# Linear attention and a cosine-gated feed-forward: Strassen's method in six token blocks instead of five, kv of two batches written by VectorE

## The chip, the cores and the metric

One NeuronCore of a Trainium2 chip. The metric is the device time of one launch in microseconds (us); the kernel before takes 818.85 us, the median of three runs (818.57 to 818.89).

## The reference

```python
def attention(q, k, v):                      # (8, 8, 576, 64): batch, head, row, d
    q_s = exp(q - max(q, -1));  q_s /= sum(q_s, -1) + 1e-9
    k_s = exp(k - max(k, 2));   k_s /= sum(k_s, 2) + 1e-9
    kv = einsum('bhsd,bhse->bhde', k_s, v)
    return einsum('bhsd,bhde->bhse', q_s, kv)

x = attention(q, k, v).transpose(0, 2, 1, 3).reshape(4608, 512)
h = x @ w_in                                 # 512 x 2048
return (h * cos(h)) @ w_out                  # 2048 x 512
```

All tensors are fp32.

## The kernel before, in words

**Tiling.** The 4608 token rows are cut into nine blocks of 512: block b = 0 to 7 holds the first 512 rows of batch b, block 8 the 64 rows left of each batch, which pass through the scratch tensor x_left. The 2048 hidden columns are 16 chunks f of 128. A block and a chunk make a unit u, 144 in all. Blocks 0 and 1 are done in turns of eight chunks (units 0 to 31); from block 2 on, u = 16 b + f.

**A unit.** fp32 operands are split into a high and a low part (type fp32r), so a product is three matmuls. A standard unit's h is 12 matmuls of 128 x 512 on TensorE (PE, L1215). Then come: ScalarE (ACT) `turns` L1221, VectorE (DVE) `rest` L1225, ACT cosine L1231, DVE `gate` L1237, ACT `hi` L1248, DVE `lo` L1254. Two units later 12 matmuls of 128 x 512 with w_out add into four PSUM banks (acc, L1458; L1451 for the first six units). w_in lies in SBUF as 16 tiles w_i (or w_io), high and low.

**Strassen.** In blocks from SB = 4 on, two units (u, u + 1) make a pair, and `products()` (from L1285) forms both h from seven products in Winograd's form, each of six matmuls of 128 x 256 (L1330). Products 0 and 1 go into the bank pb ("T1" and "B11"). ACT copies pb into the two halves of h (`seed`, L1349) and to SBUF (`p5_out`, L1353), and DVE adds p5 twice (`add_12` L1356, `add_22` L1359) between products: add_12 reads what product "T2" has finished and must read it before "T3" adds to the same half; add_22 stands between "T3" and "T4". `x_parts()` (from L919) makes the sums of x that the products need: minus L944, high and low parts L931 to L962. In a standard block x's low part is L1080.

**Sums of w_in.** `combine(a)` (from L1379) makes the sums of chunks 2a and 2a + 1: DVE L1397 to L1412, split by ACT L1416 and DVE L1420, and stores them with copies of the plain quarters in a DRAM tensor `combined` (L1389, L1391, L1424). The eight combines are listed from unit 32 on, one per four units. Each Strassen block loads 28 pieces of 512 KB back (L1298), two products per piece, into a ring of eight w_i tiles that are free by then.

**Attention.** For a batch b and a pair of heads p: k's softmax (L690 to L718), kv on PE (L767, 20 matmuls for one p), the reciprocal of its sums on DVE (L784, L787), then the 128 x 128 tile of two kv blocks. In batches 0 and 1, POOL zeroes the tile (L799) and ACT writes two 64 x 64 blocks (L804); in later batches DVE writes kvt in one instruction with a mask (`kv_norm`, L791), and ACT and DVE split it. x is PE L1044 with ACT L1058 and L1078 behind it.

**Order.** Every step goes into a plan, and the list ORDER (L59 on) is the order of all steps, written as numbers. Each engine and the DMA queue on SyncE (SP) works its own instructions in that order, and waits in it where data or a tile isn't ready. The h ring has two banks, the intermediate ring r2 three tiles.

Of the kernel before, what the change touches and what calls it, by code (L numbers as in the profile page):

```python
# [49 lines left out]
    SB=4,  # L50
# [9 lines left out]
0 1 2 3 12 4 31 7 28 13 14 20 21 80 8 9 81 74 82 15 16 83 75 24 25 34 76 84 35 85 10 11 142 77 36 78 26 27 37 44 79 45  # L60
5 6 38 92 46 86 47 29 30 94 42 52 39 48 22 23 143 40 87 49 160 161 105 54 88 41 55 50 144 311 312 313 93 43 64 56 89
106 57 95 96 97 17 18 19 156 51 98 32 33 90 100 65 53 58 101 99 66 179 180 107 59 91 67 108 330 331 102 72 162 319 109
117 157 317 318 320 112 60 321 119 68 322 110 118 163 61 323 130 145 69 328 62 314 315 316 111 324 70 63 146 113 203
204 71 120 325 334 158 121 147 73 164 326 181 159 332 122 165 114 125 123 355 356 357 131 333 126 338 182 132 347 339
358 359 124 133 327 127 166 340 148 183 341 134 149 137 167 342 335 140 141 135 184 138 336 337 343 185 150 139 136
205 349 350 186 151 344 360 168 223 224 206 243 244 361 329 173 174 152 345 207 362 153 351 208 187 366 353 369 370
363 154 367 368 169 155 209 364 192 225 352 196 197 346 354 365 193 103 104 348 287 288 194 226 210 263 264 377 170
175 216 217 211 227 188 256 257 379 228 171 189 378 229 172 190 380 230 176 381 191 231 382 177 245 383 212 198 213
302 303 246 178 195 115 116 371 384 199 236 237 202 214 789 790 247 265 385 248 266 513 514 200 218 579 580 201 249
128 129 388 267 222 389 783 784 785 372 219 232 215 278 279 220 250 552 553 373 221 390 391 268 238 251 233 392 374  # L70
269 394 270 242 395 375 234 376 289 258 393 290 235 252 291 398 239 253 271 400 292 254 240 259 241 399 280 255 401
# [12 lines left out]
853 636 681 652 667 682 1151 1152 1153 637 683 653 704 705 656 550 551 854 684 668 820 805 685 669 806 654 670 655 671
709 710 807 843 866 867 674 821 822 686 687 693 1466 1467 823 688 689 824 920 724 921 694 672 695 673 696 922 690 844
692 725 923 691 697 845 855 702 701 726 700 711 735 706 712 713 727 707 708 728 846 856 736 868 857 698 703 719 720
847 869 699 743 714 715 737 729 848 738 739 879 880 731 744 730 732 858 859 751 894 895 721 924 716 1160 717 718 745
881 882 733 1161 746 734 1162 752 747 1163 742 925 1164 753 1154 1155 1156 754 740 926 759 741 860 928 929 870 861 755
927 871 872 873 767 875 874 760 883 748 1165 896 897 750 876 1173 761 942 943 749 762 722 723 1174 768 758 884 930 931
769 756 885 825 763 886 757 764 887 1175 770 775 898 888 889 899 771 890 765 900 766 776 1180 1167 932 777 1176 933  # L90
778 1177 826 936 937 779 1157 901 1170 772 774 903 773 934 935 904 891 782 780 781 947 948 1171 1172 902 941 905 1168
1169 938 906 1178 939 1158 1159 1166 909 944 1181 1182 1179 945 946 962 910 911 1000 912 1001 940 913 963 952 953 1183
964 892 893 1002 965 949 914 1003 950 951 1004 973 1052 1053 915 1197 1208 954 1198 1199 966 957 958 969 974 1200 1201
981 967 975 1005 976 955 956 977 862 863 1184 989 968 982 959 983 960 961 1185 1211 1212 970 990 971 1006 991 984 972
1007 1186 980 1202 1010 1011 978 992 1012 985 877 878 1203 1014 1015 1019 986 979 993 987 1204 1013 1027 1020 1016
1017 1021 1187 1209 1210 1205 988 1028 1008 1009 1206 1188 1207 1022 1189 1054 1018 1219 1220 994 1055 1023 918 919
995 1234 1235 1056 1035 1024 1190 1057 1221 1222 1058 1059 1029 1060 1030 1061 1026 1512 1036 1031 1064 1065 1191 1025
1037 1513 1514 1043 1213 1038 1412 1413 1214 1034 1039 1044 1066 1032 1068 1069 1067 1045 1521 1073 1070 1071 1215
1223 1033 1104 1105 1216 1042 1236 1237 1046 1217 1040 1108 1074 1047 1041 1081 1048 1218 1062 1063 1075 1049 1264
1265 1072 1109 1082 1076 1110 998 999 1224 1111 1083 1249 1250 1112 1084 1080 1113 1192 1077 1114 1225 1115 1238 1118  # L100
1119 1089 1193 1194 1085 1251 1252 1086 1120 1226 1195 1227 1090 1097 1078 1091 907 908 1239 1079 1122 1123 1121 1240
1088 1124 1125 1098 1253 1092 1093 1116 1117 1196 1099 1127 1087 1094 1290 1291 1095 1096 1128 1522 1228 1100 1230
1231 1292 1126 1523 1101 1524 1129 1229 1130 1293 1294 1135 1131 1295 1132 1296 1133 1297 1241 1136 1242 1102 1143
1243 1103 1245 1244 1254 1137 1302 1246 1255 1134 1138 1518 1144 1515 1516 1517 1266 1267 1300 1301 1519 1520 1268
1525 1528 1298 1299 1534 1541 1139 1256 1145 1288 1289 1140 1257 1142 1535 1269 1304 1305 1141 1303 1146 1258 1306
1307 1147 1260 1536 1150 1259 1537 1148 1270 1286 1287 1538 1149 1531 1529 1530 1526 1271 1309 1542 1543 1273 1261
1362 1310 1315 1274 1272 1308 1275 1311 1276 1312 1363 1279 1313 1314 1539 1532 1533 1527 1540 1324 1280 1281 1364
1544 1282 1318 1283 1325 1319 1320 1284 1326 1232 1233 1365 1335 1327 1558 1569 1316 1317 1366 1285 1559 1560 1328
1561 1562 1343 1336 1329 1337 1572 1573 1367 1338 1330 1339 1331 1545 1332 1546 1333 1547 1344 1351 1321 1368 1322
1323 1369 1570 1571 1345 1563 1346 1334 1277 1278 1352 1342 1372 1373 1340 1353 1347 1354 1564 1374 1381 1341 1355  # L110
1375 1565 1574 1378 1379 1350 1348 1382 1349 1376 1377 1575 1414 1415 1389 1383 1247 1248 1416 1384 996 997 1566 1356
1370 1371 1380 1417 1390 1567 1385 1358 1359 1391 1576 1357 1106 1107 1397 1418 1656 1657 1419 1420 1548 1568 1392
1388 1549 1580 1581 1421 1393 1422 1577 1398 1658 1659 1386 1405 1578 1387 1582 1583 1423 1399 1396 1400 1406 1401
1394 1426 1427 1407 1550 1395 1408 1551 1424 1425 1435 1552 1579 1553 1618 1619 1409 1584 1404 1595 1596 1436 1554
1428 1402 1429 1585 1977 1437 1432 1433 1443 1438 1586 1597 1598 1403 1439 1555 1556 1451 1444 1470 1410 1978 1979
1471 1472 1473 1430 1431 1434 1474 1445 1411 1707 1708 1446 1475 1633 1634 1452 1447 1476 1453 1587 1440 1589 1477
1454 1459 1599 1480 1481 1482 1455 1600 1441 1662 1663 1986 1442 1460 1980 1981 1982 1987 1988 1483 1989 1601 1486
1487 1990 1450 1448 1620 1621 1449 1461 1557 1462 1991 1489 1456 1484 1485 1588 1463 1590 1457 1478 1479 1999 1602
1490 1604 1593 1458 1594 2000 1603 2001 1605 1491 1608 1622 1492 1497 1493 1635 1636 1623 1609 1464 1624 1610 1505
# [1592 lines left out]
```

## Time and profile before

| | |
|---|---|
| median of three runs | 818.85 us |
| profiled execution | 817.74 us |
| its span, first to last instruction | 816.0 us |
| PE busy | 794.2 us, 97% |
| DVE busy | 636.6 us, 78% |
| ACT busy | 536.1 us, 66% |
| POOL busy | 43.3 us, 5% |
| granted clock of PE | 1.000 of 2.4 GHz |

The profiled execution is one run of its own: 1.7 us of it lie outside the span, and it is 1.1 us shorter than the median of the other three. A table of windows gives each engine's busy time in a stretch; the ends used below are starts of blocks, as the trace has them (block 2 from 219.20, block 3 from 308.30, block 4 from 394.20, block 5 from 471.60 to 558.90 us). The waits view lists, for one engine, what ended its idle time. The chain is followed back from the last instruction.

### The profile page before, as it was taken

What the parts mean: (1) busy time and instruction counts of PE and PEld (TensorE: products, weight loads), DVE (VectorE), ACT (ScalarE), POOL (GpSimd) and SP (SyncE); (2) the same over time, 40 slices, a digit from 0 to 9 for tenths busy, and PEclk for the clock granted to TensorE, in tenths of its full rate; (3) what the DMA queues carried; (4) which work ended last, traced back from release to release, by engine and by line L of the source; (5) the groups of instructions that cost most, each with busy time, mean ns of one, the idle gap of its engine ahead of it and who ended that gap; (6) DMA issues with size and microseconds to landing.
All of it is one profiled execution on the core that took longest, in us unless ns stands there. A gap on an engine that the chain in (4) does not pass through costs nothing.

```text
span 816.0 us, 14069 instructions
## 1 busy us (share of the span) xinstructions
PE 794.2 (97%) x5028; PEld 706.4 (87%) x5028; DVE 636.6 (78%) x1108; ACT 536.1 (66%) x986; POOL 43.3 (5%) x161
## 2 busy tenths in 40 slices
PE   3899999999999999999999999999999999999997
PEld 2666888888888888888899999999999999999996
DVE  8999998888689886998787978687787646744444
ACT  5999998854656456756776767566666556645441
POOL 1300100000100020002000010002000000000000
PEclk9999999999999999999999999999999999999999
DMA  7893645535457544676889987998859665547721
GB/s 232 232 335 127 179 170 181 139 102 156 131 154 220 163 126 134 212 206 183 261 257 223 295 236 235 261 284 275 259 166 249 233 239 202 184 177 259 245 65 52
DMA packets 200070, 164.00 MB, mean 201 GB/s; under 512 B 110912, under 2 KB 172864, under 8 KB 200000
## 3 DMA queue, kind: packets, MB, share of 16 engines
q1 hardware_dynamic: 199680, 162.57, 66.0%
q8 instruction: 40, 0.66, 0.3%
q10 hardware_dynamic: 320, 0.52, 0.2%
q14 instruction: 30, 0.25, 0.1%
HBM read 128.71 MB, written 34.34 MB: 200 GB/s over the span
## 4 chain that ended last, share of the span: by engine, by line
PE 91%; DVE 3%; DMA 2%; SPq 1%; issue 1%; ACT 1%; POOL 0%; ACTq 0%; DVEq 0%; POOLq 0%
PE acc L1458 43%; PE h L1215 19%; PE h L1330 16%; PE pb L1330 6%; PE acc L1451 3%; PE x_False L1044 3%; PE kv L767 2%; DMA k<-in_k_dram 1%; DMA w_i<-combined 1%; POOL m L705 0%; DMA qload<-in_q_dram 0%; SPq L1093 0%; SPq L605 0%; SPq L624 0%; PE qt L995 0%
## 5 line engine op out<-in xcount | busy, mean ns | idle before, releaser
L1221 ACT ACTIVATE kt<-h 128x512 int32<-128x512 f32 x144 | 85.5, 596 | 119.4 <-PE h L1330 84.4
L1458 PE MATMUL acc<-w_o,ghi 128*128 128x512 f32 x504 | 150.1, 380 | 0.0
L1225 DVE SCALAR_TENSOR_TENSOR kt<-kt,h 128x512 f32<-128x512 int32 x144 | 97.9, 683 | 43.6 <-ACT kt L1221 43.1
L1215 PE MATMUL h<-x,w_i 128*128 128x512 f32 x528 | 121.7, 382 | 0.2 <-ACT x L1078 0.2
L1231 ACT ACTIVATE kt<-kt 128x512 f32<-128x512 f32 x144 | 90.0, 630 | 37.5 <-DVE kt L1225 36.8
L1215 PEld LDWEIGHTS h<-x,w_i 128*128 128x128 f32 x528 | 99.1, 189 | 15.4 <-ACT x L1078 0.6
L1237 DVE TENSOR_TENSOR kt<-kt,h 128x512 f32<-128x512 f32 x138 | 93.4, 684 | 23.5 <-ACT kt L1231 21.6
L1458 PEld LDWEIGHTS acc<-w_o,ghi 128*128 128x128 f32 x504 | 91.8, 190 | 11.0
L1458 PE MATMUL acc<-w_o,glo 128*128 128x512 f32 x252 | 95.5, 379 | 0.0
L1458 PE MATMUL acc<-w_o,w_io 128*128 128x512 f32 x360 | 91.4, 379 | 0.0
L1458 PE MATMUL acc<-w_io,ghi 128*128 128x512 f32 x280 | 83.4, 380 | 0.0
L1254 DVE TENSOR_TENSOR glo<-kt,ghi 128x512 fp32r<-128x512 f32 x98 | 67.3, 690 | 10.9 <-ACT ghi L1248 10.7
L1248 ACT CAST ghi<-kt 128x512 fp32r<-128x512 f32 x98 | 60.1, 617 | 21.5 <-PE acc L1458 10.7
L1458 PEld LDWEIGHTS acc<-w_o,w_io 128*128 128x128 f32 x360 | 64.3, 190 | 6.9
L1330 PE MATMUL h<-x,w_i 128*128 128x256 f32 x410 | 61.4, 275 | 0.8 <-DVE h L1356 0.5
L1330 PEld LDWEIGHTS h<-x,w_i 128*128 128x128 f32 x410 | 56.2, 191 | 3.2 <-DVE h L1356 0.7
L1330 PE MATMUL h<-w_i,w_i 128*128 128x256 f32 x358 | 57.2, 276 | 0.4 <-ACT h L1349 0.4
L1458 PEld LDWEIGHTS acc<-w_io,ghi 128*128 128x128 f32 x280 | 50.6, 190 | 5.8
L1215 PE MATMUL h<-x,w_io 128*128 128x512 f32 x240 | 55.0, 379 | 0.0
L1458 PEld LDWEIGHTS acc<-w_o,glo 128*128 128x128 f32 x252 | 47.6, 189 | 6.7
L1458 PE MATMUL acc<-w_io,glo 128*128 128x512 f32 x140 | 53.1, 379 | 0.0
L1330 PEld LDWEIGHTS h<-w_i,w_i 128*128 128x128 f32 x358 | 49.9, 191 | 2.6 <-ACT h L1349 0.9
(157 smaller groups left out, 1407.8 us busy)
## 6 DMA issues: line engine op xcount, KB each, us to landing
w_i<-combined SPq DMA_DIRECT2D x89, 512.0 KB, 5.0
w_io<-combined SPq DMA_DIRECT2D x51, 512.0 KB, 5.0
out_dram<-o SPq DMA_DIRECT2D x32, 256.0 KB, 3.1
k<-in_k_dram SPq DMA_DIRECT2D x14, 512.0 KB, 4.5
q<-in_q_dram SPq DMA_DIRECT2D x28, 256.0 KB, 3.3
qb<-q_rows SPq DMA_DIRECT2D x96, 72.0 KB, 3.2
q_rows<-q SPq DMA_DIRECT2D x24, 256.0 KB, 3.0
raw_i<-in_moe_w_in_dram SPq DMA_DIRECT2D x11, 512.0 KB, 5.9
```

The source lines that it names most:

```text
L767: nc.tensor.matmul(x[h * D : (h + 1) * D, odd : odd + vt.shape[1]], t[:, h, c, :], vt, start=(c == CM), stop=(c == CM - 1),)
L1044: nc.tensor.matmul(t[:, 0:HALF], a, c[:, cs] if whole else woven(c[:, cs]), start=(n == 0), stop=(n == len(parts) - 1 and not again))
L1215: nc.tensor.matmul(o, a, woven(x), start=(c == 0 and n == 0), stop=(c == KC - 1 and n == 2))
L1221: nc.scalar.activation(t, T["h", u], AF.Identity, bias=0.25, scale=1.0 / TWO_PI)
L1225: nc.vector.scalar_tensor_tensor(t.bitcast(F32), t, -TWO_PI, T["h", u], op0=ALU.mult, op1=ALU.add)
L1231: nc.scalar.activation(t, t, AF.Sin, bias=0.5 * math.pi)
L1237: nc.vector.tensor_mul(o, t, T["h", u])
L1248: nc.scalar.copy(t, T["kt", u].bitcast(F32))
L1254: nc.vector.tensor_sub(t, T["kt", u].bitcast(F32), T["gh", u].bitcast(F32))
L1330: nc.tensor.matmul(dst(), w[:, cs], x.rearrange("p a i -> p i a"), start=start and j == 0 and n == 0, stop=j == 1 and n == 2, skip_group_c ...
L1451: nc.tensor.matmul(T["acc", j], T["g", u][:, js], T["wc", "o", f][:, 0], start=first, stop=last)
L1458: nc.tensor.matmul(T["acc", j], a[:, js], woven(w), start=(first and n == 0), stop=(last and n == 2))
```

## The change

Block 3 (units 48 to 63) becomes a Strassen block, so there are six. The combines are listed at units 32, 35, 38, 41 (block 2) and 48, 50, 56, 58 (block 3). In block 3 the pairs of chunks 12 and 14 take their operands from w_i tiles in which the combine has just written the sums (DIRECT), and load no pieces. The other six pairs of block 3 load 21 pieces, into seven slots. In batches 0 and 1 kv's tile is written by `kv_norm` on DVE; the POOL and ACT steps for it are gone. The list ORDER is new from end to end.

```diff
-    SB=4,
+    KVD=((0, 0), (0, 1), (0, 2), (0, 3), (1, 0), (1, 1), (1, 2), (1, 3)),
+    SB=3,
...
         def kv_norm():
-            t = T["kvt", b, p] = sbt([P, P], F32, "kvt", f"kvt_{b}_{p}", kvt)
+            if kvt:
+                t = T["kvt", b, p] = sbt([P, P], F32, "kvt", f"kvt_{b}_{p}", kvt)
+            else:
+                t = T["kv", b, p] = sbt([P, P], F32, "kvw", f"kvw_{b}_{p}", kvw)
...
-        if b < CFG["XF"]:
+        if b < CFG["XF"] and (b, p) in CFG["KVD"]:
+            plan.add("DVE", 0.33, kv_norm, reads=[o, r], writes=[kvw])
+        elif b < CFG["XF"]:
...
+    SIDES = ((0, 1, 2), (5, 8, 9))
+    PIECES = (6, 7, 12, 13, 10, 11, 3, 4)
+    DIRECT = {12: [("w", "i", 6), ("w", "i", 7)], 14: [("w", "i", 10), ("w", "i", 11)]}
+    COMBINE = {32: 0, 35: 1, 38: 2, 41: 3, 48: 4, 50: 5, 56: 6, 58: 7}
...
-        return ("w", "i", 3 * (b % 2) + k)
+        return ("w", "i", SIDES[(b - SB) % 2][k])
...
-            far = ("w", "i", NF - 2 + u % 2)
+            far = ("w", "i", (3 if b == SB else NF - 2) + u % 2)
...
-        return ("w", "i", 6 + n % 8)
+        if n < NOP // 2:
+            return ("w", "i", 3 + n if n < 7 else 5 + n % 7)
+        return ("w", "i", PIECES[(n - NOP // 2) % 8])
...
+        direct = u - SB * NF if u - SB * NF in DIRECT else None
         for n in range(first // 2 if f == 0 else n0, n1 + 1):
+            if direct is not None:
+                continue
...
+        def source(o):
+            if direct is None:
+                return piece((first + o) // 2), (first + o) % 2
+            if o in (1, 2, 6):
+                return ("w", "i", f + o // 6), (o - 1) % 2 if o < 6 else 1
+            i, k = {3: (0, 0), 5: (0, 1), 4: (1, 0), 0: (1, 1)}[o]
+            return DIRECT[direct][i], k
+
         def operand(o):
-            t = T[piece((first + o) // 2)].rearrange("p n (h c) -> p n h c", h=2)[:, (first + o) % 2]
-            return t[:, 0], t[:, 1]
+            w, k = source(o)
+            t = T[w].rearrange("p n (h c) -> p n h c", h=2)
+            return (t[:, k, 0], t[:, k, 1]) if direct is None else (t[:, 0, k], t[:, 1, k])
...
+        def hi_there(i, x):
+            nc.scalar.copy(T[x][:, 0], T["sum", a][:, i])
+
+        def lo_there(i, x):
+            t = T[x]
+            nc.vector.tensor_sub(t[:, 1], T["sum", a][:, i], t[:, 0].bitcast(F32))
+
+        def put_there(i, x):
+            t = T[x].bitcast(F32)
+            for k, o in enumerate(((3, 5), (4, 0))[i]):
+                nc.sync.dma_start(combined[:, o0 + o], t[:, :, 2 * P * k : 2 * P * (k + 1)])
+
+        if f0 in DIRECT:
+            for i, x in enumerate(DIRECT[f0]):
+                ops = [("combined", o0 + o) for o in ((3, 5), (4, 0))[i]]
+                plan.add("ACT", 0.62, lambda i=i, x=x: hi_there(i, x), reads=C, writes=[x], due=due)
+                plan.add("DVE", 0.69, lambda i=i, x=x: lo_there(i, x), reads=C, writes=[x], due=due)
+                plan.load([0.8] * 2, lambda i=i, x=x: put_there(i, x), reads=[x], writes=ops, due=due)
+            return
...
-        if 32 <= u < SB * NF and (u - 32) % (2 * (SB - 2)) == 0 and SB <= B:
-            combine((u - 32) // (2 * (SB - 2)), when(u + 2.0))
+        if u in COMBINE:
+            combine(COMBINE[u], when(u + 2.0))
```

The names in the order's rows are those of the code, with the unit or the batch and head pair behind them (kv_1_0: batch 1, pair 0) and a buffer number last; line numbers after the change are 8 to 32 higher.

**PE, start of the program.** Before, ahead of and in unit 0's h:

```order
L1044 MATMUL x1_0_2_False_480<-qt_0_2_418,kvw_0_2_443 128x288
L767 MATMUL kv_1_0_486<-v_sb0_87,k_1_0_314 64x66 x2
L767 MATMUL kv_1_0_486<-v_sb0_87,k_1_0_314 64x65 x8
L767 MATMUL kv_1_1_499<-v_sb1_93,k_1_0_314 64x66 x2
L767 MATMUL kv_1_1_499<-v_sb1_93,k_1_0_314 64x65 x8
L1044 MATMUL x0_0_2_True_517<-qt_0_2_418,kvw_0_2_443 128x288
```

After the change, the end of unit 0's h and on:

```order
L1233 MATMUL h_0_462<-x_0_3_504,w_i0_433 128x512 x3
L1233 MATMUL h_1_546<-x_0_0_344,w_i1_489 128x512 x3
L1233 MATMUL h_1_546<-x_0_1_377,w_i1_489 128x512 x3
L1233 MATMUL h_1_546<-x_0_2_457,w_i1_489 128x512 x3
L1233 MATMUL h_1_546<-x_0_3_504,w_i1_489 128x512 x3
L775 MATMUL kv_1_0_568<-v_sb0_87,k_1_0_297 64x66 x2
L775 MATMUL kv_1_0_568<-v_sb0_87,k_1_0_297 64x65 x8
```

Batch 1's first kv products moved from ahead of h_0 to behind h_1.

**DVE, start of the program.** After the change, kv's tile of batch 0, pair 0 (kvw_0_0) is written right behind its reciprocal; before, no such row stood on DVE:

```order
L792 TENSOR_SCALAR r_0_0_316<-kv_0_0_266 128x1
L795 RECIPROCAL r_0_0_316<-r_0_0_316 128x1
L703 TENSOR_TENSOR m1_0_2_319<-mt_0_2_299 128x128
L802 SCALAR_TENSOR_TENSOR kvw_0_0_321<-kv_0_0_266,r_0_0_316,mask_83 128x128
L698 TENSOR_TENSOR mt_0_3_325<-k_0_3_193 128x256
```

The row of L802 is the one that came in.

**DVE in block 3, between the first sums of a combine and unit 56.** After the change (L1435 to L1444 are sums of w_in, L1388 and L1391 the pair's adds, L888 to L896 are q of batch 4):

```order
L1429 TENSOR_TENSOR wc_sb_175<-w_io13_1593 128x512
L888 TENSOR_REDUCE qs_4_1_3777<-q_4_1_3569 128x18
L1435 TENSOR_TENSOR wc_sb_175<-wc_sb_175 128x256
L1438 TENSOR_TENSOR wc_sb_175<-wc_sb_175 128x256
L1441 TENSOR_TENSOR wc_sb_175<-wc_sb_175 128x256
L1388 TENSOR_TENSOR h_56_3773<-h_57_3779,p5_56_3775 128x256
L892 TENSOR_SCALAR qs_4_1_3777<-qs_4_1_3777 128x18
L893 RECIPROCAL qs_4_1_3777<-qs_4_1_3777 128x18
L1272 TENSOR_TENSOR glo_54_3817<-kt_54_3726,ghi_54_3784 128x512
L896 TENSOR_TENSOR q_4_1_3569<-q_4_1_3569,qs_4_1_3777 128x1152
L1444 TENSOR_TENSOR wc_sb_175<-wc_sb_175 128x256
L1391 TENSOR_TENSOR h_57_3779<-h_57_3779,p5_56_3775 128x256
```

The same work before the change:

```order
L1403 TENSOR_TENSOR wc_sb_175<-wc_sb_175 128x256
L1406 TENSOR_TENSOR wc_sb_175<-wc_sb_175 128x256
L1409 TENSOR_TENSOR wc_sb_175<-wc_sb_175 128x256
L815 TENSOR_TENSOR kvw_4_0_3450<-kvt_4_0_3444,kvw_4_0_3450 128x128
L883 TENSOR_TENSOR q_4_0_3400<-q_4_0_3400,qs_4_0_3571 128x1152
L791 SCALAR_TENSOR_TENSOR kvt_4_1_3634<-kv_4_0_3329,r_4_0_3436,mask_83 128x128
L1412 TENSOR_TENSOR wc_sb_175<-wc_sb_175 128x256
L1237 TENSOR_TENSOR kt_54_3590<-kt_54_3590,h_54_3552 128x512
```

The pair's two adds now stand between that work and have it ahead of them.

**PE in block 3, its first pair.** After the change, product T2 (five rows of h_49), the first product of the next pair (pb_50), and the first row of T3 (h_49 again):

```order
L1362 MATMUL h_49_3276<-w_i2_539,w_i4_662 128x256
L1362 MATMUL h_49_3276<-w_i0_433,w_i4_662 128x256
L1362 MATMUL h_49_3276<-w_i2_539,w_i4_662 128x256 x2
L1362 MATMUL h_49_3276<-w_i1_489,w_i4_662 128x256
L1362 MATMUL h_49_3276<-w_i2_539,w_i4_662 128x256
L1362 MATMUL pb_50_3299<-x_3_0_2971,w_i6_774 128x256
L1362 MATMUL pb_50_3299<-w_i0_433,w_i6_774 128x256
L1362 MATMUL pb_50_3299<-x_3_0_2971,w_i6_774 128x256
L1362 MATMUL pb_50_3299<-x_3_1_3118,w_i6_774 128x256
L1362 MATMUL pb_50_3299<-w_i1_489,w_i6_774 128x256
L1362 MATMUL pb_50_3299<-x_3_1_3118,w_i6_774 128x256
L1362 MATMUL h_49_3276<-x_3_0_2971,w_i5_752 128x256
```

Standard units stood there before; now one product lies between the end of T2 and the start of T3.

## Rows read from the trace of the kernel before

**Rows 1.** The page: busy time of each engine, and the 40 slices of PE and its clock.

```profile
PE 794.2 (97%) x5028; PEld 706.4 (87%) x5028; DVE 636.6 (78%) x1108; ACT 536.1 (66%) x986; POOL 43.3 (5%) x161
...
PE   3899999999999999999999999999999999999997
...
PEclk9999999999999999999999999999999999999999
```

**Rows 2.** Waits of PE: engine, line, releaser: us in total, times, longest.

```profile
PE qt L995 <- DVE q L883: 11.2, 1, 11.2
PE kv L767 <- ACT k L718: 1.2, 1, 1.2
PE kv L767 <- DMA v<-in_v_dram: 1.0, 1, 1.0
PE kv L767 <- DMA v_sb<-in_v_dram: 0.9, 1, 0.9
...
PE h L1330 <- DVE h L1356: 0.5, 1, 0.5
PE h L1330 <- ACT h L1349: 0.4, 1, 0.4
PE h L1330 <- DMA w_i<-combined: 0.3, 1, 0.3
```

**Rows 3.** Chain, block 3's and block 4's start: start us, us, what.

```profile
308.49 5.18 PE h L1215 x24
...
395.87 0.37 ACT h L1349
396.23 0.04 issue
396.28 1.60 PE h L1330 x12
...
404.78 1.34 PE h L1330 x12
```

**Rows 4.** Windows: start:end length, PE, PEld, DVE, ACT, POOL busy, clock, DMA share, GB/s.

```profile
44.70:124.50 79.80, 79.80 (x362) 60.55 (x363) 76.66 (x120) 78.02 (x131) 3.88 (x6) 1.00 0.59 193
...
219.20:308.30 89.10, 89.10 (x492) 78.37 (x491) 75.95 (x133) 51.06 (x87) 5.41 (x26) 1.00 0.58 166
308.30:394.20 85.90, 85.90 (x545) 75.56 (x544) 73.60 (x125) 59.19 (x97) 5.93 (x26) 1.00 0.68 192
394.20:471.60 77.40, 76.95 (x529) 71.96 (x526) 64.11 (x115) 53.73 (x108) 3.18 (x14) 1.00 0.87 253
471.60:558.90 87.30, 87.30 (x646) 81.38 (x645) 70.14 (x121) 58.91 (x115) 5.07 (x26) 1.00 0.87 258
```

**Rows 5.** Chain, last pieces of the start.

```profile
39.77 0.31 ACT kvw L804
40.10 0.60 ACT kt L1221
...
44.70 2.81 PE acc L1451 x6
```

**Rows 6.** Timeline of PE: kv of batch 1 ahead of unit 0's h.

```profile
29.68 1.40 PE L767 MATMUL kv<-v_sb,k 128*64 128x66 f32 x40 [0.93 <-DMA v_sb<-in_v_dram]
```

**Rows 7.** Groups of DVE, ACT and POOL: busy us, mean ns | idle before.

```profile
L1359 DVE TENSOR_TENSOR h<-h,p 128x256 f32<-128x256 f32 x40 | 17.2, 431 | 32.8 <-PE h L1330 32.6
...
L1237 DVE TENSOR_TENSOR kt<-kt,h 128x512 f32<-128x512 f32 x138 | 93.4, 684 | 23.5 <-ACT kt L1231 21.6
...
L791 DVE SCALAR_TENSOR_TENSOR kvt<-kv,r,mask 128x128 f32<-128x128 f32 x24 | 8.3, 346 | 0.4
...
L1349 ACT COPY h<-pb 128x256 f32<-128x256 f32 x80 | 28.4, 364 | 15.7 <-DVE kt L1237 10.7 <-PE pb L1330 4.8
...
L1353 ACT COPY p<-pb 128x256 f32<-128x256 f32 x40 | 15.0, 374 | 4.6 <-PE pb L1330 2.0 <-DVE glo L1254 1.4 <-DVE h L1359 1.2
...
L804 ACT ACTIVATE kvw<-kv,r 64x64 f32<-64x64 f32 x16 | 5.0, 310 | 0.7 <-POOL kvw L799 0.6
```

More of the change, by code (lines that the diff above doesn't have):

```diff
@@ L1361, in reads @@
         def reads(o):
-            return xr + [piece((first + o) // 2)]
+            return xr + [source(o)[0]]
         A, us = CFG["step"], 0.675
@@ L1662, in linear_attention_then_cos_gated_mlp @@
                 splits.pop(f)()
-        if 32 <= u < SB * NF and (u - 32) % (2 * (SB - 2)) == 0 and SB <= B:
-            combine((u - 32) // (2 * (SB - 2)), when(u + 2.0))
+        if u in COMBINE:
+            combine(COMBINE[u], when(u + 2.0))
     for u in (NU - 4, NU - 3):
```

315 rows, old and new, of the table ORDER are left out of this document.

## The prediction

> **What bounds the kernel now.** First the page. PE is busy 97% of the span, and both its busy slices and its clock stand at 9 from the third slice to the last but one; DVE has 78%, ACT 66% [rows 1]. So after a start that isn't PE's, the time is the sum of PE's work, and a change counts by what it takes from that sum or adds to PE's waits. Second the waits of PE [rows 2]. The one large wait, 11.2 us, and those on kv all lie in the first 45 us; behind 46 us the view has three waits of 1.2 us in all, every one on a Strassen product (L1330): for the add L1356, the seed L1349, and a piece from `combined`. Third the windows [rows 4]. From 44.70 us on PE is busy for whole blocks without a gap, while DVE's share goes from 83% (64.11 of 77.40) up to 96% (76.66 of 79.80), and the DMA share reaches 0.87. So DVE at 96% beside a PE without gaps is something this kernel does already, but with standard units only; with Strassen pairs the trace shows 83% at most.
>
> **The prices on PE.** The chain gives 5.18 us for 24 matmuls of 128 x 512, so 0.216 us each, and 1.34 us for 12 of 128 x 256, so 0.112 us each [rows 3]. A standard pair of units has 24 wide ones for h: 5.18 us. A Strassen pair has 7 x 6 = 42 narrow ones: 42 x 0.112 = 4.70 us. That is 0.48 us less per pair, and 8 pairs change: **-3.84 us**. The matmuls with w_out stay.
>
> The narrow matmul's row is what decides this sign: a saving of 12.5% in columns is left with 9% in time because 0.112 us is a little over half of 0.216. The Trainium skill ("TensorE: Matmul & The Clock Gate", section "Back-to-back issue gap") gives two rules: an isolated gap of N/2.4 + 2.5 ns, and, for a stream of weight loads and matmuls in a real kernel, about 81 ns at 128 columns and 131 ns at 512. By the second rule, with an estimated 98 ns at 256 by a straight line between its figures, a Strassen pair would take 42 x 0.098 = 4.1 us and a standard one 24 x 0.131 = 3.1 us, and the change would lose about 1 us per pair. The rows of this trace, a stream with a new weight load for each matmul, are at the first rule and not at the second.
>
> **The change part by part.**
>
> *Work added beside PE, block 3.* Each pair has two adds at 0.431 us on DVE, two seeds at 0.364 and a p5 copy at 0.374 us on ACT [rows 7]: in 8 pairs DVE 16 x 0.431 = 6.9 us, ACT 8 x 1.10 = 8.8 us. PE's time of the block becomes 85.9 - 3.8 = 82.1 us. ACT comes to 59.2 + 8.8 = 68.0 of 82.1, 83% [rows 4]: it stays hidden, as it did at 78.02 of 79.80 in the first blocks. DVE comes to 73.6 + 6.9 = 80.5 of 82.1, 98% [rows 4]. That is 2% above the highest share that the trace shows beside a PE without gaps. If 96% is the most, the block lasts 80.5 / 0.96 = 83.9 us, 1.8 more than PE needs; if the new list lets DVE run ahead into blocks 2 and 4 (85% and 83% now), nothing. Between 0 and 1.8 I take **+0.6**, nearer to nothing, because three tiles of r2 and the two units between h and its use leave DVE some room. The order shows where it would be lost: ahead of pair 56's adds stand, in one run, sums of w_in and parts of batch 4's q.
>
> *New waits of PE.* A product that needs an add or a seed waits unless other PE work lies between. At unit 64, the start of block 4, one product lies there (0.67 us), and the chain goes over the seed, 0.37 us of ACT [rows 3]; PE's wait is 0.4 [rows 2]. The new order has the same tight start twice, at units 48 and 64, and one product between T2 and T3 at unit 48. A free DVE does its add of 0.431 inside 0.67; behind one 0.684 instruction [rows 7] it is 0.5 late. So for the added start: nothing at best, the seed's 0.4 and two late adds, 1.4, at worst; I take the seed, **+0.4**.
>
> *x of block 3.* The sums of x replace L1080's parts. They fall into block 2, where DVE has 13 us to spare (75.95 of 89.10 [rows 4]). Nothing; if they don't fit, they are late for unit 48 by one instruction, 0.7 us, inside the range.
>
> *Combines and pieces.* The eight combines stay, four in each of blocks 2 and 3. Block 3 loads 21 pieces more. Block 5 moves 258 GB/s at a share of 0.87 [rows 4], so a piece of 512 KB (0.524 MB) takes 0.524 x 0.87 / 258 GB/s = 1.77 us of all DMA engines. In SP's new order 11 of the 21 stand ahead of the first store of block 2's output, 10 behind it. Block 2: 0.58 x 89.1 + 11 x 1.77 = 71.2 of 89.1, 0.80; block 3: 0.68 x 85.9 + 10 x 1.77 = 76.1 of 82.1, 0.93 at most. The pieces are issued some four units ahead, so I take nothing; a late one cost 0.3 [rows 2], ten of them 3. The pairs of chunks 12 and 14 wait for DVE's low parts in place of a load; those stand one to two pairs ahead of the product, so nothing, and 0.7 if one instruction's time is missing.
>
> *Batch 4's attention* now uses one PSUM bank, as that of the batches behind it did, whose blocks show no wait of PE on attention [rows 2]. Nothing.
>
> *kv of batches 0 and 1.* 16 instructions of 0.310 us leave ACT, 8 memsets leave POOL, 8 of 0.346 us come to DVE [rows 7]. One of ACT's lies on the chain right ahead of unit 0's first step, 0.31 us at 39.77 [rows 5]. In the same move batch 1's first kv leaves the place ahead of unit 0's h: 1.40 us of work and a wait of 0.93 [rows 6], and the order of DVE and ACT in the start is another. The PE work only moves; what can be won is idle time, 44.7 - 28.8 = 15.9 us if all were gone. The three waits that the moves touch are 1.0 on v's load, 0.9 on v_sb's, 0.8 on kvw [rows 2]: 2.7 at best. At worst DVE carries four of the new instructions ahead of unit 0's gate, 4 x 0.346 = 1.4 more, and nothing else gives. What ends the start is DVE and ACT up to the first matmul with w_out at 44.70 [rows 5], so most of a PE wait removed comes back at the next wait for them. I take **-0.8**, a third of the best case. Behind 44.70 us PE has no gaps, so this passes to the end unchanged.
>
> *The end* (blocks 7 and 8) has the same work in PE's order; nothing.
>
> **The sum.** -3.84 - 0.8 + 0.4 + 0.6 = -3.6 us. The profiled execution would go from 817.74 to 814.1 us. It lies 1.1 us below the median of the runs, so the median is forecast at 818.85 - 3.6 = **815.2 us**.
>
> **The rivals.** About 0.2%, 1.6 us, is what a measurement of this kernel can tell from no change: faster is below 817.2, slower above 820.5.
>
> *The start gives its best case.* All three waits go, and block 3 loses only the seed: -3.84 - 2.7 + 0.4 = -6.1, 812.7 us. For it: unit 0's h has less ahead of it on PE and ACT. Against: the chain there runs through DVE. Chance 0.15.
>
> *Given back.* The start gives nothing, DVE holds at 96%, and the tight start costs its worst: -3.84 + 1.8 + 1.4 = -0.6, 818.2 us: no difference to be measured. For it: 16 new places where PE hangs on DVE. Chance 0.16.
>
> *DVE becomes block 3's bound: slower.* A pair's adds sit between two products, so DVE can't be late and catch up behind: where it is, PE stops, h comes later, and DVE then idles for it. What decides is the share that DVE reaches. To be slower by over 1.6 us, with the start's 0.8 and the seed's 0.4, block 3 must last 3.84 + 0.8 - 0.4 + 1.6 = 5.8 us longer than 82.1, so DVE at 80.5 / 87.9 = 92% or less. At 90% the block takes 89.4 us, 7.3 more: -3.84 - 0.8 + 0.4 + 7.3 = +3.1, 821.9 us. For it: in blocks 4 and 5 DVE's idle time stands mostly before these adds, 32.8 us before L1359 over 40 of them [rows 7], and the share there is 83%. Against: that idle time is there because DVE has less to do; the start blocks run at 96%, and the new list puts the adds by hand. Chance 0.11.
>
> *Narrow matmuls dearer in a stream.* Should the price be other in block 3 than in blocks 4 to 8, where 40 pairs' 1680 run at 0.112 [rows 3], each 0.01 us more costs 336 x 0.01 = 3.4 us; at 0.129 the change comes to -3.6 + 5.7 = +2.1, 820.9 us, slower. Nothing in the trace speaks for it. (The Trainium skill's second rule would have this sign; no row meets it.) Chance 0.01. That the change doesn't do what it says can be left out: the new order has the products of 128 x 256 in block 3.
>
> **How the numbers follow.** The forecast has 0.57, the best start 0.15, given back 0.16, DVE as bound 0.11, dearer matmuls 0.01. The range takes in the best start and the given-back case: **812.6 to 818.8 us**; of the terms' ends added up, -3.84 - 2.7 = -6.5 and -3.84 + 1.4 + 1.4 + 1.8 = +0.8, it leaves out the corners. Faster 0.57 + 0.15 = 0.72; same 0.16; slower 0.12.
>
> **What would show it.** Right: windows of block 3 near 82 to 83 us with PE busy throughout and DVE over 95%; the first w_out matmul about 0.8 us earlier than 44.70; waits of PE on L1356, L1359 and L1349 (new line numbers) of 2 to 3 us in all. Wrong: a block 3 of 86 us or more with PE waiting on DVE's adds, a start that ends at 45 us or later, or waits on pieces from `combined` above 1 us.

## The result, and the profile after

The kernel after takes 811.68 us (median of 6 runs, 810.47 to 813.44) beside 818.87 us before (6 runs, 818.57 to 820.45). The ratio is 0.9909 with a 95% interval of 0.9897 to 0.9921: 7.2 us faster, twice the 3.6 forecast, and 0.9 us below the lower end of the range. The profiled executions are 811.02 and 817.74 us, 6.7 us apart.

The page after, answering to [rows 1]: busy time of each engine, and the slices of PE and its clock.

```profile
PE 789.3 (98%) x5172; PEld 707.2 (87%) x5172; DVE 647.3 (80%) x1140; ACT 545.9 (67%) x1004; POOL 42.7 (5%) x153
...
PE   3899999999999999999999999999999999999997
...
PEclk9999999999999999999999999999999999999999
```

PE is still the bound, with 4.9 us less busy time, though it has 144 instructions more. DVE got 10.7 us more and ACT 9.8.

The waits of PE after, whole span, answering to [rows 2]:

```profile
PE qt L1013 <- DVE q L896: 11.6, 1, 11.6
PE kv L775 <- DMA v<-in_v_dram: 2.4, 1, 2.4
PE kv L775 <- DMA v_sb<-in_v_dram: 1.0, 1, 1.0
PE kv L775 <- ACT k L726: 0.4, 1, 0.4
```

All four are in the start. The three waits of Strassen products that stood in [rows 2] are gone, and in this execution none came in their place, though there are now 48 pairs' products instead of 40 (a second execution has one, see after_again). One wait in the start, on a load of v, has grown from 1.0 to 2.4 us.

The windows after (start:end length, busy time of PE, PEld, DVE, ACT and POOL, clock, DMA share, GB/s), answering to [rows 4]; the ends are the starts of unit 32, block 3, unit 64, unit 80:

```profile
216.90:299.00 82.10, 82.10 (x460) 72.23 (x460) 72.50 (x127) 49.70 (x88) 4.14 (x9) 1.00 0.68 193
299.00:390.20 91.20, 91.20 (x729) 84.21 (x727) 86.37 (x155) 66.49 (x124) 7.82 (x44) 1.00 0.88 259
390.20:468.20 78.00, 78.00 (x533) 72.69 (x532) 63.77 (x112) 54.68 (x109) 2.71 (x9) 1.00 0.88 260
```

The same view in shorter windows of block 3:

```profile
330.00:350.00 20.00, 20.00 (x131) 18.39 (x131) 19.69 (x33) 14.44 (x25) 0.00 (x0) 1.00 0.90 287
350.00:370.00 20.00, 20.00 (x141) 18.57 (x141) 19.69 (x39) 14.27 (x33) 0.61 (x2) 1.00 0.84 215
```

Block 3 holds more work in its window than before, because the new list cuts the blocks elsewhere. DVE is busy 95% of it, and 98% for 40 us on end, and PE has no gap. The prediction's doubt whether Strassen pairs let DVE be that busy is answered: they do, with little room left (after_again, dve_4).

The chain of the kernel after, in order of time, at the start of block 3 (start us, us, what), answering to [rows 3]:

```profile
299.12 1.34 PE pb L1362 x12
300.45 2.59 PE acc L1509 x12
303.05 1.34 PE h L1362 x12
304.38 0.67 PE pb L1362 x6
305.06 2.25 PE h L1362 x18
```

The narrow matmuls cost what they cost in the other blocks, 1.34 / 12 = 0.112 us, and behind product B11 (the second half of pb) stands a whole unit of w_out matmuls, 2.59 us, where ACT's seeds have time.

**Where the 6.7 us are.** From the trace's PE rows one can add up idle time: what lies from one matmul's start to the next beyond the usual distance of its width (0.216, 0.112 us and so on; gaps under 0.03 us left out). PE's work, the matmuls counted at these distances, falls from 780.2 to 776.4 us: -3.84, as forecast; the narrow ones of the new block have the same 0.112 us as the others. The time until the first matmul and the idle up to 100 us together fall from 29.9 to 28.4: -1.5. Idle behind 100 us falls from 5.1 to 4.0: -1.1. What is left, -0.3, is in the small gaps and behind the last matmul.

That the start ends sooner is seen best at unit 0's `rest` on DVE. The timeline of DVE before:

```profile
40.76 0.68 DVE L1225 SCALAR_TENSOR_TENSOR kt<-kt,h 128x512 f32<-128x512 int32 x1
```

and after:

```profile
36.45 0.67 DVE L1243 SCALAR_TENSOR_TENSOR kt<-kt,h 128x512 f32<-128x512 int32 x1
```

It is 4.3 us earlier. Not all of it is won, since batch 1's first kv is now done behind it. The chain of the start has changed too. Before, it ran through DVE and ACT up to 44.70 us [rows 5]; in the kernel after, from v's landing on, it is PE's own work:

```profile
16.13 6.81 DMA v<-in_v_dram
...
38.28 2.79 PE h L1233 x12
41.06 1.72 PE acc L1502 x4
```

In the second execution (after_again) it still goes over DVE and ACT from 23.9 to 33.7 us, though PE does the same work at nearly the same times: the two are close to a tie.

### The profile page after: what moved, and what is told of

Same layout as the page of the kernel before. It is cut to its first block, busy times and chain, and to the rows that moved or that the text cites. A ratio compares the mean times of both kernels' runs of the same rounds, so it can differ in the third digit from the quotient of the medians.

```text
span 809.2 us, 14405 instructions
## 1 busy us (share of the span) xinstructions
PE 789.3 (98%) x5172; PEld 707.2 (87%) x5172; DVE 647.3 (80%) x1140; ACT 545.9 (67%) x1004; POOL 42.7 (5%) x153
## 4 chain that ended last, share of the span: by engine, by line
PE 97%; SPq 2%; DMA 1%; issue 0%; DVE 0%
PE acc L1509 44%; PE h L1362 20%; PE h L1233 16%; PE pb L1362 8%; PE x_False L1062 3%; PE acc L1502 3%; PE kv L775 2%; DMA v<-in_v_dram 1%; PE x_True L1062 0%; PE qt L1013 0%; SPq L632 0%; SPq L583 0%; SPq L574 0%; SPq L613 0%; SPq L663 0%
## 5 line engine op out<-in xcount | busy, mean ns | idle before, releaser
L1509 PE MATMUL acc<-w_o,ghi 128*128 128x512 f32 x456 | 136.4, 381 | 0.0
L1233 PE MATMUL h<-x,w_i 128*128 128x512 f32 x396 | 92.1, 383 | 0.0
L1509 PEld LDWEIGHTS acc<-w_o,ghi 128*128 128x128 f32 x456 | 82.2, 190 | 9.5
L1509 PE MATMUL acc<-w_o,glo 128*128 128x512 f32 x228 | 86.4, 379 | 0.0
L1233 PEld LDWEIGHTS h<-x,w_i 128*128 128x128 f32 x396 | 74.1, 189 | 12.2 <-issue 0.7
L1362 PE MATMUL h<-x,w_i 128*128 128x256 f32 x502 | 75.9, 276 | 0.0
L1362 PEld LDWEIGHTS h<-x,w_i 128*128 128x128 f32 x502 | 69.3, 191 | 3.0 <-DVE h L1388 0.6
L1362 PE MATMUL h<-w_i,w_i 128*128 128x256 f32 x428 | 68.2, 276 | 0.0
L1272 DVE TENSOR_TENSOR glo<-kt,ghi 128x512 fp32r<-128x512 f32 x90 | 61.1, 682 | 8.9 <-ACT ghi L1266 8.6
L1266 ACT CAST ghi<-kt 128x512 fp32r<-128x512 f32 x90 | 55.3, 620 | 18.8 <-DVE kt L1255 10.9
L1362 PEld LDWEIGHTS h<-w_i,w_i 128*128 128x128 f32 x428 | 59.4, 191 | 2.2 <-ACT h L1381 0.2
L1362 PE MATMUL pb<-x,w_i 128*128 128x256 f32 x314 | 50.9, 275 | 0.0
```

Of the source, the lines that this page charges most:

```text
L1233: nc.tensor.matmul(o, a, woven(x), start=(c == 0 and n == 0), stop=(c == KC - 1 and n == 2))
L1266: nc.scalar.copy(t, T["kt", u].bitcast(F32))
L1272: nc.vector.tensor_sub(t, T["kt", u].bitcast(F32), T["gh", u].bitcast(F32))
L1362: nc.tensor.matmul(dst(), w[:, cs], x.rearrange("p a i -> p i a"), start=start and j == 0 and n == 0, stop=j == 1 and n == 2, skip_group_c ...
L1509: nc.tensor.matmul(T["acc", j], a[:, js], woven(w), start=(first and n == 0), stop=(last and n == 2))
```

## The experiments

The last column but one is the time to the first matmul plus idle up to 100 us, from each run's own profile; the last is the idle behind 100 us.

| run | median us | ratio to before (95%) | start us | idle later us |
|---|---|---|---|---|
| before | 818.87 | | 29.9 | 5.1 |
| after | 811.68 | 0.9909 (0.9897 to 0.9921) | 28.4 | 4.0 |
| kvd_alone | 819.26 | 1.0006 (0.9997 to 1.0015) | 31.3 | 4.7 |
| kvd_undone | 815.60 | 0.9958 (0.9942 to 0.9973) | 32.1 | 3.8 |
| head_new | 822.79 | 1.0044 (1.0027 to 1.0061) | 29.4 | 13.5 |
| tail_new | 823.29 | 1.0053 (1.0038 to 1.0068) | 30.7 | 10.0 |
| two_covers | 817.42 | 0.9982 (0.9972 to 0.9992) | 30.6 | 4.4 |
| start64_bare | 812.32 | 0.9914 (0.9898 to 0.9930) | 29.1 | 4.2 |
| v_early | 811.50 | 0.9901 (0.9885 to 0.9918) | 28.4 | 4.0 |
| dve_4 | 812.54 | 0.9915 (0.9900 to 0.9929) | 27.6 | 5.8 |
| head_new2 | 816.05 | 0.9962 (0.9948 to 0.9976) | 27.8 | 5.5 |
| kvd_undone2 | 815.97 | 0.9960 (0.9946 to 0.9974) | 33.8 | 4.4 |
| dve_16 | 819.49 | 1.0006 (0.9997 to 1.0015) | 27.4 | 12.8 |
| after_again | 811.60 | 0.9904 (0.9890 to 0.9918) | 28.8 | 5.0 |

In three of these profiles a stretch of the start ran at the lower level of PE's clock (0.50 in the clock column): kvd_alone from 25.0 to 28.4 us, tail_new from 24.3 to 27.7, start64_bare from 23.5 to 26.9. Their start column holds what that cost.

**kvd_alone.** The kernel before, with one edit of the change: kv of batches 0 and 1 on DVE, at the places that ACT's steps had in the list.

```diff
-        if b < CFG["XF"]:
+        if b < CFG["XF"] and (b, p) in CFG["KVD"]:
+            plan.add("DVE", 0.33, kv_norm, reads=[o, r], writes=[kvw])
+        elif b < CFG["XF"]:
```

> The kernel before, with kv of batches 0 and 1 written by VectorE, every other step where it stood. Theory L (the new list of steps removed waits of PE; the kv edit itself is worth little): within 0.5 us of the kernel before, about 818.5 us, and PE idle in the first 100 us as before (18.7 us beside 16.9 after the change). Rival K (the kv edit is what shortened the start): 1.0 to 1.5 us faster, about 817.5 us.

No difference (+0.4 us, interval -0.2 to +1.2). Alone, the edit is worth nothing that can be measured: rival K falls here.

**kvd_undone.** The kernel after without that edit; POOL's and ACT's steps stand where `kv_norm` stood.

```diff
-    KVD=((0, 0), (0, 1), (0, 2), (0, 3), (1, 0), (1, 1), (1, 2), (1, 3)),
+    KVD=(),
```

> The kernel after, with kv of batches 0 and 1 written by POOL and ScalarE again, at the same places of the new list. Theory L: within 0.5 us of the kernel after, 811.2 to 812.2 us. Rival K: the start's 1.0 to 1.5 us come back, about 813 us.

3.9 us slower than after: neither theory. In the new list the edit is worth far more than the 1.5 us of rival K. Two of PE's waits, whole span, in this run:

```profile
PE x_False L1073 <- ACT kvw L826: 1.9, 2, 1.1
PE qt L1024 <- ACT kvw L826: 1.6, 1, 1.6
```

and the timeline of ACT shows why the first kv tile is late there:

```profile
16.09 1.13 ACT L894 ACTIVATE q<-qload 128x512 f32<-128x512 f32 x2
17.13 0.61 ACT L826 ACTIVATE kvw<-kv,r 64x64 f32<-64x64 f32 x2
```

It stands behind an exponential of q in ACT's queue and ends at 17.74 us. In the kernel after, DVE writes the same tile at 16.58, right behind the reciprocal, and has it by 16.93. (In the kernel before, PE's waits for this tile were `PE x_False L1044 <- ACT kvw L804: 0.8, 2, 0.4`.)

```profile
16.31 0.16 DVE L795 RECIPROCAL r<-r 128x1 f32<-128x1 f32 x1
16.39 0.27 DVE L703 TENSOR_TENSOR m<-mt 128x128 f32<-128x128 f32 x1
16.58 0.35 DVE L802 SCALAR_TENSOR_TENSOR kvw<-kv,r,mask 128x128 f32<-128x128 f32 x1
```

**kvd_undone2.** The same, but both steps right behind the reciprocal in the list, ahead of what else ACT has there.

```diff
 DVE kv_inv
+POOL kv_frame, ACT kv_f32
 ...
-POOL kv_frame, ACT kv_f32
```

> The kernel after with kv of batches 0 and 1 written by POOL and ScalarE, and those two steps right behind the reciprocal in the list, earlier than in the run before (kvd_undone). Theory L2 (in kvd_undone ScalarE's own queue was behind at the old places, so kv came 1 to 2 us late three times; earlier places repair most of it): 812 to 814 us. Rival K2 (ScalarE has no room at all in this list's start, so the edit is needed): 814.5 to 816 us.

The time is rival K2's: 4.4 us slower than after (815.97 beside 811.60), no better than before the move. But the move reached only the later tiles. The first one stands behind the same exponential of q as in kvd_undone, because the list has that exponential ahead of the reciprocal:

```profile
15.92 1.14 ACT L894 ACTIVATE q<-qload 128x512 f32<-128x512 f32 x2
16.96 0.62 ACT L826 ACTIVATE kvw<-kv,r 64x64 f32<-64x64 f32 x2
```

So ACT has no room for these 16 instructions at the two sets of places tried; that it has none anywhere isn't shown. (The 33.8 us of this profile can't be set beside kvd_undone's 32.1: PE's clock rose at 22.8 us here and at 16.4 there, see the last section.) Together with kvd_alone: the edit and this list need each other.

**head_new and head_new2.** The kernel before with the kv edit and the new list for the start alone, first up to unit 16's h, then up to unit 32's, the old list behind it. The edit is to ORDER alone:

```diff
-all steps in the old order
+the steps that stand in the new list up to that matmul, in the new order
+all other steps in the old order
```

> The kernel before with the kv edit and the new list up to the first matmuls of unit 16 (about 124 us); from there the old list and five Strassen blocks. Theory L: the start's idle of PE falls by 1.5 us, 817.0 to 817.6 us. Rival N (the idle differs between single executions and has nothing to do with the list): 818.3 to 819.3 us.

head_new is 4.0 us slower. Behind the seam PE waits 4.6 us, up to 133.7 us, for a gate of DVE, which stands behind work on weights, k's softmax and q that ACT and DVE do one after the other; that the cut piled this work up there is argued from the lists and not shown by a run. The wait has a second price: PE's clock fell to its lower level in it, at 132.1 us, and rose at 138.9, so the 12 matmuls behind the wait are 0.427 us apart instead of 0.216, 2.6 us more.

```profile
132.00:139.00 7.00, 5.31 (x13) 4.26 (x14) 5.58 (x8) 1.81 (x3) 0.00 (x0) 0.51 0.00 0
```

Together that is 7.2 of the 8.4 us by which the later idle exceeds that of before. A list can't be cut anywhere; this run tells nothing of the start but its own 29.4 us.

> The kernel before with the kv edit and the new list up to the first matmuls of unit 32 (217 us, where the two lists have done nearly the same work: 0 us of VectorE's work missing, 3 us ahead); from there the old list. Theory L2 (the start's gain comes from the new list together with the kv edit, and is about 2 us, not 0.8): 816.4 to 817.4 us, PE's first start and idle up to 100 us together 28.4 to 29.3 us, beside 30 to 30.7 with the old list. Rival N (the start's idle differs between executions and not between lists): 818.3 to 819.3 us.

With a cut at which DVE is ahead and not behind, the kernel is 2.7 us faster than before (interval 2.0 to 4.3), with five Strassen blocks and the old list for the rest. Its profile has 27.8 us of start. This is the gain of the new list up to block 2, the start in the main: theory L2, and by its time a little better than that. The old list with kv on ACT has 29.9, 30.7 and 30.6 us in three runs (before, tail_new, two_covers), mean 30.4; the new list with kv on DVE has 27.4 to 29.4 in eight, mean 28.4. So 2.0 by profiles, also without tail_new and start64_bare (30.3 and 28.3), and 2.7 by the time of this run.

**tail_new.** The kernel before with the new list from unit 64 on, seam at block 4's start.

```diff
-all steps in the old order
+the steps that stand in the new list ahead of product T1 of unit 64, in the old order
+all other steps in the new order
```

> The kernel before with the new list from unit 64 on (block 4), same work. Theory L: the three waits of PE on Strassen products at 396, 565 and 617 us (0.61 + 0.67 + 0.43 us) are gone, 817.2 to 818.0 us. Rival N: 818.5 to 819.3 us.

Slower by 4.5 us, neither theory. Two of the three old waits are gone (those at 565 and 617 us); the seed's 0.6 is still there, at 400 us, and the seam has new ones (0.8 us on either side of it, and others up to 711). It doesn't tell whether the list removes waits; the next two do.

**two_covers.** The kernel before with two moves.

```diff
+L1330 MATMUL pb_64 (T1, B11)
 L767  MATMUL kv_5 (80 matmuls)
-L1330 MATMUL pb_64 (T1, B11)
 L1330 MATMUL h_65 (T2)
...
-L712  TENSOR_TENSOR k_7 (DVE)
 L1356 TENSOR_TENSOR h_96 (DVE, add_12 of pair 96)
+L712  TENSOR_TENSOR k_7 (DVE)
```

> The kernel before with two moves in its list: batch 5's kv (80 matmuls) moved from ahead of block 4's first pair to behind its product B11, where the product T2 waits for ScalarE's seeds (0.61 us of PE idle at 396 us); and one subtraction of batch 7's k softmax on VectorE moved from ahead of pair 96's add_12 to behind it, where PE waits (0.67 us at 565 us). Theory C (a short cover in the list is what costs there, and other PE work in the gap removes it): PE's idle behind 380 us falls from 3.3 to about 2.0 us, 817.3 to 818.0 us. Rival M (the wait moves to the next product): no change, 818.5 to 819.2 us.

Theory C: 1.6 us faster (interval 0.7 to 2.3). The chain of this run at the place:

```profile
393.98 2.51 PE kv L777 x80
...
398.13 0.94 PE pb L1340 x6
399.07 2.13 PE h L1340 x18
```

ACT's seed, which ended PE's wait there in [rows 3], is off the chain. A smaller wait of 0.3 us, for p5, comes behind kv; the gap of 0.67 us at 565 us is gone as well. The run moves both covers at once, so its 1.6 us isn't split between them.

**start64_bare.** The kernel after with the reverse of it at unit 64.

```diff
 L1362 MATMUL pb_64 (T1, B11)
-L1509 MATMUL acc_48_1<-w_io14,ghi_62 and glo_62
 L1362 MATMUL h_64 (B21)
 L1362 MATMUL h_65 (T2)
+L1509 MATMUL acc_48_1<-w_io14,ghi_62 and glo_62
```

> The kernel after with one move in its list: a quarter of unit 62's matmuls with w_out (3 of 128 x 512, 0.65 us) taken from between product B11 of unit 64 and the next product, to behind T2. Theory C: PE waits for the seeds again, 0.4 to 0.7 us, 811.9 to 812.6 us. Rival M: no change beside the kernel after, 811.2 to 812.0 us, because what was moved covers another wait.

The times can't tell it from the kernel after (812.32 beside 811.68, within the intervals), but the wait is back. The chain of this run, in order of time:

```profile
390.86 1.55 PE pb L1372 x12
392.41 0.02 issue
392.44 0.36 ACT h L1391
392.80 0.04 issue
392.85 1.60 PE h L1372 x12
```

PE stands from 392.4 to 392.85 us for ACT's copy of 0.36, as in [rows 3], where the same piece of chain was in the kernel before. Theory C by the trace alone.

**v_early.** The kernel after, the load of v for batch 0, pair 2 issued ahead of two others.

```diff
+load v_0_2
 load raw_o0 (w_out, chunk 0)
 load raw_i1 (w_in, chunk 1)
-load v_0_2
```

> The kernel after with one move in its list: the load of v for batch 0, pair 2 issued two transfers of 512 KB earlier (ahead of the first w_out chunk and the second w_in chunk). Theory V (the start ends when that load lands; PE waits 2.4 us for it): the wait goes and 1 to 2.4 us with it, 809.3 to 810.7 us. Rival W (DVE and the next loads hold the start just behind it, so another wait takes its place): 811.0 to 812.0 us.

No difference from after (811.50 beside 811.68), rival W by the time: 810.4 to 811.8 in four runs, beside 810.4 to 813.4 in ten of the kernel after. The wait on v is gone from the profile, and the start is 28.4 us as before it. What takes its place isn't shown: in this execution PE's clock rose only at 20.5 us (last section), and the x matmuls ahead of v's kv end at 22.5 us instead of 20.6 for that reason.

**dve_4 and dve_16.** The kernel after, with one instruction of DVE doubled in four or in all sixteen units of block 3.

```diff
             nc.vector.tensor_sub(t, T["kt", u].bitcast(F32), T["gh", u].bitcast(F32))
+            if u in (48, 52, 56, 60):
+                nc.vector.tensor_sub(t, T["kt", u].bitcast(F32), T["gh", u].bitcast(F32))
```

> The kernel after with the low part of the gate's result written twice in units 48, 52, 56 and 60: 4 x 0.68 = 2.7 us more on VectorE in block 3, nothing else. Theory S (DVE at 95% there still has 4.8 us to spare and is not the bound): under 0.8 us more, 811.5 to 812.5 us. Rival D (DVE is at its limit in block 3): the whole 2.7 us, about 814.4 us.

> As dve_4, in all 16 units of block 3: 10.9 us more on VectorE there. With 4.8 us to spare, theory S2 (DVE's idle time in block 3 can be used almost whole, work beyond it costs its full time): 10.9 - 4.8 = 6.1 us and the 0.9 us seen with four, 817.5 to 819 us. Rival D2 (half of any added work is paid from the first microsecond): 5 to 5.5 us, about 817 us. Rival D (all of it): 822.5 us.

2.7 us more work cost 0.9 us, 10.9 us cost 7.9 (819.49 beside 811.60). The 0.9 is a difference of medians whose runs overlap (811.85 to 812.77 beside 810.36 to 813.44), the 7.9 is clear. S's picture holds roughly: a third of the first 2.7 us is paid, and 7.0 of the next 8.2. dve_16 is 0.5 us above what S2 gave, so the usable part of DVE's 4.8 us of idle is nearer 3 than 4. In dve_16 the bound has changed sides; windows of its block 3 (columns as above) and its waits of PE in that stretch:

```profile
330.00:350.00 20.00, 18.34 (x114) 16.14 (x113) 19.66 (x33) 13.47 (x23) 0.00 (x0) 1.00 0.85 280
350.00:370.00 20.00, 19.13 (x132) 16.89 (x131) 19.90 (x38) 13.19 (x28) 0.31 (x1) 1.00 0.73 189
```

```profile
PE h L1364 <- ACT h L1383: 1.6, 4, 0.6
PE h L1364 <- DVE h L1390: 1.4, 2, 1.3
PE h L1364 <- DVE h L1393: 1.2, 2, 0.7
```

PE waits for the pair's adds and for the seeds behind DVE's late work, as the prediction's slower rival had it. The kernel after can take about 3 us more of DVE's work before all of it is paid (an estimate: 10.9 - 7.9).

**after_again.** The kernel after, unchanged.

> The kernel after, unchanged, beside the three others on one chip, as their reference and for a second profile of its start: 811 to 812.5 us. If the start's idle differs between executions of one list by under 1 us, first start and idle up to 100 us are again 27.6 to 29.1 us; rival N has 30 us in one of them.

811.60 us and a start of 28.8. One wait of 0.8 us on a seed at 364 us (PE h L1362 on ACT h L1381) is in this execution and not in the first: idle behind 100 us differs by 1 us between executions of one kernel. The wait lies in block 3, and its chain shows how DVE's lack of room there becomes PE's:

```profile
359.17 2.58 DMA qb<-q_rows
...
362.47 0.66 DVE kt L1255
363.13 0.02 issue
363.16 0.36 ACT h L1381
363.52 0.04 issue
363.56 0.94 PE h L1362 x6
```

DVE waits for a transfer of q, its gate comes late, ACT's seed comes behind the gate, and PE stands.

## Why the prediction was wrong

**PE's work: right.** -3.84 us by 8 pairs of 42 x 0.112 beside 24 x 0.216; the trace has these numbers of matmuls at these distances. The rule of the Trainium skill that would have made narrow matmuls dear in a stream ("TensorE: Matmul & The Clock Gate", section "Back-to-back issue gap") is met by no row of the new block either: 0.112 us again.

**The start: the mechanism right, the size wrong.** The step was "I take -0.8, a third of the best case". Measured: -1.5 in the profiled pair, -2.0 as the mean of the profiles, -2.7 in head_new2, which is the best case. Two things failed in the step. It bounded the gain by the three waits that the moves touch, and let DVE's and ACT's queues give most of it back ("most of a PE wait removed comes back at the next wait for them"); but the new list also takes work from these two queues ahead of unit 0, which the step mentioned as "another order" and didn't price. In the trace ACT has 68 instructions ahead of unit 0's `turns` before and 55 after (12 of the difference are kv's), DVE 97 ahead of unit 0's `rest` before and 93 after, its four new ones included. `rest` came 4.3 us earlier, and of the three waits only part moved as the best case had it: v's grew from 1.0 to 2.4, v_sb's from 0.9 to 1.0, kvw's 0.8 is gone. And the step counted the kv edit as 1.4 us more on DVE at worst. The runs show the edit as the condition of the gain: without it this list's start has 32.1 us instead of 28.4 (kvd_undone), with the chain on ACT from 30 us on, and alone it gives nothing. An instruction taken from an engine whose queue is behind is worth the wait of those who need it, here 1.1 and 1.6 us, not its own 0.31 us.

**"At unit 64 one product lies there (0.67 us)": wrong.** No product lay there. In the old list T2 stood directly behind B11, so nothing covered the seed; that is why PE waited. The row ahead of those in [rows 3] is the bank of T1 and B11:

```profile
394.30 1.55 PE pb L1330 x12
```

It ends at 395.85, ACT's seed starts at 395.87, and PE's next row, 396.28, is T2. From the misread cover came the step "so for the added start I take the seed, +0.4". The new list has 2.59 us of w_out matmuls at unit 48 and a quarter unit at unit 64 in that place. So the term isn't +0.4, but the old waits' 0.61 and 0.67 us less. These two gaps stand in every profile that has the old list there unmoved (before, kvd_alone, head_new and head_new2: 0.61, and 0.59 to 0.67), and in none of the kernel after's list unmoved; two_covers takes both out, start64_bare brings the first back.

**DVE in block 3, "+0.6": not wrong by what is shown.** It is 0 in the first profile, where DVE reached 98% beside a PE without gaps (the step took 96% as the most the trace had shown), and 0.8 in the second (after_again). That DVE would be near its limit was right; dve_16 shows what lies behind the edge. One reading in the same place was off: DVE's lowest share in [rows 4] is block 5's 80% (70.14 of 87.30), not 83%; no term hangs on it.

**Combines, pieces, the end: right.** No wait of PE on any of them; the DMA share of block 3 is 0.88, below the 0.93 that was given as the most. The split of the pieces was off: 5 and not 11 are issued in block 2's window, whose share is 0.68 instead of 0.80. **Attention, "nothing":** 0 in the first profile; the 0.8 us of after_again starts at a late transfer of q.

**The sum.** -3.84, -2.0 for the start, -0.7 for the later waits (mean of the profiles without moved covers, seams or added work: 4.9 with the old list in two, 4.2 with the new in five, which spread from 3.8 to 5.0) and -0.3 of small gaps make -6.8, beside 7.2 measured; the rest is within the interval of 1 us on either side. The start and the seed were taken too small and on the wrong side by the same habit: each added or moved piece was priced for the wait it could bring, and the list's removals were not looked for. By these two the forecast was 1.2 and 1.1 us too slow, and by DVE's +0.6 up to 0.6.

**The rivals.** The start's best case, at 0.15, was nearest for the start, but it still carried +0.4 for the seed: 812.7, 1 us too slow. DVE as the bound has the mechanism right, as dve_16 shows, and needs about 3 us of work more than there is.

## What to carry to other kernels

Before pricing a wait from the trace, read in the order what stands between the producer and the consumer: a wait that exists may be a missing cover that a new order fills, and then the term has the other sign. When a whole list is new, look for the waits that it removes with the same care as for those that it adds, place by place along the waits view. A small edit that moves work between engines and the order made for it can't be priced apart: each alone gave nothing or a loss in the start here, both together some 2 us. And a wait of PE can cost more than its length: behind head_new's 4.6 us the matmuls ran at the lower clock for another 2.6.

## What was not expected of the hardware

The same x matmuls of batch 0 (fp32, 128 x 288) ran at two speeds in different executions, and the clock column of the windows, 1.00 in both, doesn't tell them apart. PE's timeline in the kernel after:

```profile
17.11 1.24 PE L1062 MATMUL x_False<-qt,kvw 128*128 128x288 f32 x4
```

and in v_early:

```profile
17.73 2.29 PE L1072 MATMUL x_False<-qt,kvw 128*128 128x288 f32 x4
```

Start to start they are 0.24 us apart in the one and 0.48 in the other. What differs is PE's clock, and the column hides it: the trace's record of the granted clock has its first entry, full speed, at 15.00 us in the kernel after and at 20.52 us in v_early, and the column shows 1.00 also ahead of the first entry, where the record is empty. In v_early the distance falls from 0.48 to 0.24 with that entry. So it does in the other profiles whose record starts behind the first x matmul (from 18.15 us in kvd_alone to 22.85 in kvd_undone2). That 0.48 belongs to the lower of the two levels, 1.2 GHz, is seen where the record does have an entry for it, in start64_bare:

```profile
23.50:26.85 3.35, 3.35 (x13) 2.78 (x12) 3.32 (x8) 2.44 (x8) 0.00 (x0) 0.50 1.09 340
```

In that stretch two x matmuls of the same shape are 0.48 us apart again, and behind it 0.24.

The start hides most of this. Where the clock rises late, the wait for v behind these matmuls is short or gone (0.3 us in dve_4 beside 2.4), and `rest` of unit 0 isn't later for it: 35.4 us in dve_4 and dve_16, 36.5 in v_early, 36.45 and 36.48 in the two of the kernel after. PE's first matmul stands at 11.2 to 11.6 us in all 14 profiles; why the clock rises at 15.0 us in one and at 22.8 in another stays open, and no run here was made for it.
